# An RWKV and GELU-MLP kernel: the wait between two groups of products on one PSUM tile, through GpSimd instead of a drain

## Chip, core and metric

The kernel runs on one core of a Trainium2 chip. The metric is the device time of one execution in microseconds (us). Before the change its median is 507.57 us over three runs (505.82 to 508.35).

## What is computed

A linear recurrence over 768 time steps for 4 batches and 8 heads of 48 dimensions, and behind it a two-layer MLP with GELU over all 3072 tokens (384 to 2048 to 384). In float32, cut to what matters:

```
for t in range(S):
    kt, vt, rt = k[:, :, t], v[:, :, t], r[:, :, t]
    cur = einsum('bhd,bhe->bhde', u * kt, vt)
    y[:, :, t] = einsum('bhd,bhde->bhe', rt, state + cur)
    state = w * state + einsum('bhd,bhe->bhde', kt, vt)
h = x @ w_in                       # x: y with the heads side by side
out = (0.5 * h * (1 + erf(h / sqrt(2)))) @ w_out
```

## The kernel before

The sequence is cut into 6 chunks of 128 steps, the heads into 4 pairs, so there are 24 groups, a pair in a chunk each. A chunk is halved in time. A group's output is the sum of two kinds of products in PSUM tile Y: those of the old state with r (`old`, line 427) and those of the new keys, that is of the masked scores `Am` with v (`new`, line 437). The scores themselves are products of keys with r (`scores`, line 408, into PSUM tile A); the first eight groups are "direct" and take the step's own key in a second set (`own`, the same line). The products k*v that a state gains over each half go into the upper columns of Y (`gains`, line 419; in the first four groups into another tile). VectorE makes the new state out of the old one and the gains (`state`, line 460), ScalarE and VectorE take the output out of Y as a high and a low part (`keep`, lines 479 and 480).

The MLP runs beside it: per chunk 16 steps, each with 9 big products of 128x512 into tile `Hp` (line 554), GELU on ScalarE (583, 584), a remainder on VectorE (585) and 9 big products into tiles `O` (line 596). Each weight is split into a high part `wh` and a low part `wl` on ScalarE and VectorE (lines 330 to 342), in the first chunk's steps.

After the first four groups, a group's small products come in "visits" between the MLP's big ones (`products`): a visit does `old` and `new` for the group g and `scores` and `gains` for the next group f. A class `Plan` sets the order of all instructions on all engines when the kernel is built, from estimated times and due times; one visit is one entry of it on TensorE, so within a visit the order is as the function `go` writes it. All engines run their queues in that order.

`old` takes its weights from rows that cross over: row half j^h of the array writes into bank h. `new` takes row half h into bank h. So two row halves of the array would write into one bank of Y, and `new` begins with a drain of TensorE (line 433), which waits until all that was issued to TensorE is done. Each `old`, `scores`, `gains` and `new` of a visit is 16 matrix products, 32 records in the trace (8 products for the gains of the last chunk's groups). GpSimd (POOL) multiplies the natural-layout tiles `Nb` of the next group (lines 379, 381, 391), VectorE the transposed ones `Tb` (line 375) and sums rows (line 394); `Nb` and `Tb` have two buffers each and are loaded through SP's queue.

Of the kernel before, what the change touches and what calls it, by code (L numbers as in the profile page):

```python
# [18 lines left out]
B, H, S, D = 4, 8, 768, 48  # L19
# [4 lines left out]
NP = H // 2  # L24
# [3 lines left out]
HALF = 64  # L28
# [17 lines left out]
class Plan:  # L46
# [9 lines left out]
    def add(self, eng, ns, at, fn, r=(), w=()):  # L56
        n = len(self.ops)
        deps = set()
        for x in r:
            deps.add(self.writer.get(x))  # L60
            self.readers.setdefault(x, []).append(n)
        for x in w:
            deps.add(self.writer.get(x))
            deps.update(self.readers.pop(x, ()))
            self.writer[x] = n
        deps -= {None, n}
        self.ops.append((eng, ns, at, fn, deps))
        self.reads.append(set(r))
# [65 lines left out]
def rwkv_gelu_mlp(tc, rkT, rkv, wuT, uN, wmlp, r, k, vT, w, u, out):  # L134
    nc = tc.nc
    with ExitStack() as ctx:
# [11 lines left out]
        AA = psp.tile([128, 2, 512], F32, name="A")  # L148
        YU = psp.tile([128, 2, 512], F32, name="Y")
# [3 lines left out]
        UE = pso.tile([128, 2, 512], F32, name="UE")  # L153
# [194 lines left out]
        U0 = NB * HALF  # L348
        SLOTS = NP + 1
        quarter = lambda x: slice(64 * x, 64 * x + D)  # L350
        heads = lambda x: slice(D * x, D * x + D)
        times = lambda h: slice(64 * h, 64 * h + 64)

        class Group:
            def __init__(g, gi):
                g.gi, g.c, g.p = gi, gi // NP, PAIRS[gi % NP]
                s, i = slot(gi), gi % 2
                g.direct, g.more = gi < DIRECT, g.c < NCH - 1
                g.t, g.T = T[s], f"T{s}"
                g.n = N[s]  # L360
                g.R, g.K, g.V = f"Nr{s}", f"Nk{s}", f"Nv{s}"
                g.kn, g.vn = (g.n[:, 0], g.n[:, 1]) if gi < NP else (g.n[:, 1], g.n[:, 2])
                g.am, g.AM = Am[i], f"Am{i}"
                g.kb, g.KB = KB[i], f"KB{i}"
                g.sums, g.CS = cs[i], f"cs{i}"
                g.x, g.X = (AE, ["O0", "O1"]) if gi < NP and i else (AA, ["A0", "A1"])
                g.y, g.Y = YU, ["Y0", "Y1"]
                g.u, g.U, g.u0 = (UE, ["O2", "H"], i * 256) if gi < NP else (YU, g.Y, U0)
                g.s = [St[0][:, gi % SLOTS], St[1][:, i], St[0][:, (gi + NP) % SLOTS]]
                g.S = [[f"Sa{gi % SLOTS}{x}" for x in range(2)], [f"Sb{i}{x}" for x in range(2)],  # L370
                       [f"Sa{(gi + NP) % SLOTS}{x}" for x in range(2)]]
# [31 lines left out]
        def scores(g, keys=None, col=0):  # L403
            for b in range(NB):
                for h in range(2):
                    for x in range(2):
                        k_ = (g.t[:, 1] if keys is None else keys)[quarter(x), b, times(h)]
                        nc.tensor.matmul(g.x[times(h), x, col + b * HALF:col + (b + 1) * HALF], lhsT=k_,  # L408
                                         rhs=g.t[quarter(x), 0, b, times(h)], start=True, stop=True)

        def own(g):
            scores(g, g.kb, U0)


        def gains(g):
            for b in range(NB):
                for x in range(2):
                    for h in range(2 if g.more else 1):
                        nc.tensor.matmul(g.u[quarter(x), h, g.u0 + b * D:g.u0 + (b + 1) * D], lhsT=g.kn[times(h), b, heads(x)],  # L419
                                         rhs=g.vn[times(h), b, heads(x)], start=True, stop=True)  # L420

        def old(g):
            for b in range(NB):
                for j in range(2):
                    for h in range(1 if g.c == 0 else 0, 2):
                        l = quarter(j ^ h)
                        nc.tensor.matmul(g.y[quarter(j), h, b * HALF:(b + 1) * HALF], lhsT=g.s[h][l, b, :],  # L427
                                         rhs=g.t[l, 0, b, times(h)], start=(b == 0 and not spreads(g)), stop=False,
                                         skip_group_check=True)


        def new(g):
            nc.tensor.drain()
            for b in range(NB):
                for j in range(2):
                    for h in range(2):
                        nc.tensor.matmul(g.y[quarter(j), h, b * HALF:(b + 1) * HALF], lhsT=g.vn[times(h), b, heads(j ^ h)],  # L437
                                         rhs=g.am[times(h), j ^ h, b, :], stop=True, skip_group_check=True,
                                         start=(g.c == 0 and h == 0 and b == 0 and not spreads(g)))


        spreads = lambda g: g.c == 0 and g.p < 3
# [48 lines left out]
        def first_group(gi):  # L491
            g = Group(gi)
            prepare(g)
            add("pe", 600, LATER, lambda: scores(g), r=[g.T], w=g.X)
            add("pe", 600, LATER, lambda: own(g), r=[g.T, f"{g.KB}0", f"{g.KB}1"], w=g.X)
            add("pe", 500, LATER, lambda: (setattr(plan, "hold", True), gains(g)), r=[g.K, g.V], w=g.U)
            state(g, 0, LATER)
            select(g, diag2, "diag", U0)
            select(g, past2, "past", 0)
            if spreads(g):  # L500
                add("pe", 1000, LATER, lambda: gaps(g), r=["spread", "x3h", "x3l"], w=g.Y)
            add("pe", 1000, LATER, lambda: (old(g), new(g)), r=[g.T, g.V, g.AM] + g.S[1], w=g.Y)
            keep(g, LATER)
            state(g, 1, LATER)

        def products(g, f):


            r, w, ns = [], [], 0
            if g:  # L510
                r += [g.T, g.V, g.AM] + g.S[0] + g.S[1]
                w += g.Y
                ns += 1200
            if f:
                r += [f.T, f.K, f.V] + ([f"{f.KB}0", f"{f.KB}1"] if f.direct else [])
                w += f.X + f.U
                ns += 1300 if f.direct else 850

            def go():
                if g:  # L520
                    old(g)
                if f:
                    scores(f)
                    if f.direct:
                        own(f)
                if g:
                    new(g)
                if f:
                    gains(f)

            add("pe", ns, LATER, go, r=r, w=w)
# [175 lines left out]
        for n, x in enumerate(LOADS):  # L707
            at = 10 * n + 1
# [29 lines left out]
        def step_at(m):  # L738
            return FIRST + STEP * min(m, 5 * NJ) + STEP_LAST * max(m - 5 * NJ, 0)

        for G in range(NSTEP + 1):
# [8 lines left out]
            if G % 4 == 0 and G // 4 + NP < NG:  # L750
                gi = G // 4 + NP + 1
                at = step_at(4 * (gi - 1 - NP)) + GROUP_DUE
# [12 lines left out]
        with tc.If(plain[0] < 2 * LP * NP):  # L765
# [5 lines left out]
            g = general.enter_context(tc.tile_pool(name="g", bufs=2))  # L771
# [76 lines left out]
```

## Time and profile before

| | |
|---|---|
| median of 3 runs | 507.57 us (505.82 to 508.35) |
| span of the profiled execution | 507.7 us |
| TensorE products (PE) busy | 486.0 us, 96% |
| TensorE weight loads (PEld) busy | 390.1 us, 77% |
| VectorE (DVE) busy | 243.0 us, 48% |
| ScalarE (ACT) busy | 205.5 us, 40% |
| GpSimd (POOL) busy | 71.6 us, 14% |
| mean granted TensorE clock | 0.971 of full speed |

The span is the time from the first to the last instruction of one profiled execution, on which all rows below rest. Records of products overlap, since they are pipelined and their ends are modelled; distances from start to start are the surer measure. "Idle before" is the time for which an engine had nothing to do, and after the arrow stands what ended it.

### The profile page before, as it was taken

How to read it: one execution, taken by the hardware profiler on the slowest of the kernel's cores; microseconds unless marked ns; L12 is line 12 of the kernel's file. 1: busy time of each engine (PE TensorE's matmuls, PEld its weight loads, DVE VectorE, ACT ScalarE, POOL GpSimd, SP SyncE). 2: the span in 40 equal slices, each digit the busy share in tenths (PEclk: the TensorE clock that was granted, in tenths of full speed). 3: DMA queues.
4: the chain of work that ended last, by engine and by line, in shares of the span. 5: the costliest groups of instructions: out<-in, count | busy, mean ns of one | idle time of the engine just before them, and what ended most of it. 6: DMA issues, size and time to landing. Idle time of an engine off the chain costs nothing.

```text
span 507.7 us, 11458 instructions
## 1 busy us (share of the span) xinstructions
PE 486.0 (96%) x5009; PEld 390.1 (77%) x5009; DVE 243.0 (48%) x366; ACT 205.5 (40%) x435; POOL 71.6 (14%) x80
## 2 busy tenths in 40 slices
PE   7879899999999999999999999999999999999995
PEld 5767677777787787777787787787787787888884
DVE  5869899998345344625254434253433231211111
ACT  3448567755442442442433443433442423322221
POOL 4220101033022022301121120220220200000000
PEclk9568999999999999999999999999999999999999
DMA  7954736622303113403023403033403000100001
GB/s 222 247 196 135 253 118 217 196 87 88 124 24 96 52 43 96 146 1 94 8 88 94 144 3 94 1 94 94 143 5 95 0 13 10 64 1 0 0 1 66
DMA packets 13190, 43.85 MB, mean 86 GB/s; under 512 B 1808, under 2 KB 2192, under 8 KB 13136
## 3 DMA queue, kind: packets, MB, share of 16 engines
q1 hardware_dynamic: 13136, 43.07, 27.3%
q8 instruction: 41, 0.67, 0.6%
q14 instruction: 13, 0.11, 0.1%
HBM read 36.38 MB, written 4.72 MB: 81 GB/s over the span
## 4 chain that ended last, share of the span: by engine, by line
PE 80%; DVE 11%; issue 3%; DMA 3%; ACT 1%; POOL 0%; SPq 0%; DVEq 0%; ACTq 0%; POOLq 0%
PE Hp L554 35%; PE O L596 34%; PE Y L437 3%; PE A L408 3%; PE Y L427 2%; DVE wa L338 2%; DVE wl L342 2%; DVE wa L336 1%; DMA raw<-in_wmlp_dram 1%; PE Y L419 1%; PE Y L596 1%; DVE Am L465 1%; DMA Nb<-in_rkv_dram 1%; DVE gl L585 1%; DVE Tb L375 1%
## 5 line engine op out<-in xcount | busy, mean ns | idle before, releaser
L554 PE MATMUL Hp<-xx,wh 128*128 128x512 f32 x576 | 168.1, 399 | 1.7 <-ACT gf L584 1.0
L585 DVE TENSOR_TENSOR gl<-gf,gh 128x512 fp32r<-128x512 f32 x95 | 71.4, 752 | 193.5 <-ACT gf L584 193.3
L583 ACT ACTIVATE gh<-Hp 128x512 fp32r<-128x512 f32 x95 | 56.9, 599 | 227.7 <-PE Hp L554 227.5
L554 PEld LDWEIGHTS Hp<-xx,wh 128*128 128x128 f32 x576 | 107.0, 189 | 27.9 <-ACT wh L340 1.8
L554 PE MATMUL Hp<-xx,wl 128*128 128x512 f32 x288 | 84.4, 400 | 1.7 <-DVE wl L342 1.7
L596 PE MATMUL O<-gh,wh 128*128 128x512 f32 (+1 forms) x285 | 82.2, 395 | 0.2 <-issue 0.2
L596 PE MATMUL O<-gh,wl 128*128 128x512 f32 (+1 forms) x285 | 80.7, 390 | 0.0
L596 PE MATMUL O<-gl,wh 128*128 128x512 f32 (+1 forms) x285 | 80.7, 390 | 0.0
L554 PEld LDWEIGHTS Hp<-xx,wl 128*128 128x128 f32 x288 | 54.0, 189 | 16.7 <-DVE wl L342 4.1
L596 PEld LDWEIGHTS O<-gh,wh 128*128 128x128 f32 x285 | 52.5, 188 | 13.0 <-issue 0.7
L596 PEld LDWEIGHTS O<-gl,wh 128*128 128x128 f32 x285 | 52.6, 188 | 11.7
L596 PEld LDWEIGHTS O<-gh,wl 128*128 128x128 f32 x285 | 52.5, 188 | 11.6
L584 ACT ACTIVATE gf<-Hp 128x512 f32<-128x512 f32 x96 | 56.9, 593 | 0.0
L379 POOL TENSOR_TENSOR Nb<-Nb 128x384 f32<-128x384 f32 x16 | 18.5, 1159 | 258.1 <-DMA Nb<-in_rkv_dram 215.8
L399 ACT ACTIVATE Am<-diag,cs 128x64 f32<-128x64 f32 x128 | 33.5, 343 | 5.1 <-DVE cs L394 5.0
L381 POOL TENSOR_TENSOR Nb<-Nb,WN 128x384 f32<-128x384 f32 x20 | 27.0, 1349 | 44.2 <-DMA Nb<-in_rkv_dram 42.9
L375 DVE TENSOR_TENSOR Tb<-Tb,E 112x1024 f32<-112x1024 f32 x20 | 25.4, 1269 | 2.0 <-DMA Tb<-in_rkT_dram 1.8
L460 DVE SCALAR_TENSOR_TENSOR Sb<-Sa,E,Y 48x192 f32<-48x192 f32 x40 | 16.5, 413 | 15.4 <-ACT xx L479 9.3
L394 DVE TENSOR_REDUCE cs<-Nb 128x8 f32<-128x384 f32 x16 | 8.8, 552 | 25.5 <-POOL Nb L391 25.5
L479 ACT CAST xx<-Y 112x512 fp32r<-112x512 f32 (+1 forms) x18 | 10.6, 587 | 25.0 <-PE Y L419 17.4
L391 POOL TENSOR_TENSOR Nb<-Nb,u_sb 128x384 f32<-128x384 f32 x16 | 17.7, 1107 | 0.1
L330 ACT ACTIVATE wa<-raw 128x768 f32<-128x768 f32 x16 | 14.6, 912 | 6.5 <-DMA raw<-in_wmlp_dram 4.7
(122 smaller groups left out, 398.8 us busy)
## 6 DMA issues: line engine op xcount, KB each, us to landing
raw<-in_wmlp_dram SPq DMA_DIRECT2D x16, 768.0 KB, 5.0
Nb<-in_rkv_dram SPq DMA_DIRECT2D x16, 576.0 KB, 5.2
Tb<-in_rkT_dram SPq DMA_DIRECT2D x20, 448.0 KB, 3.9
out_dram<-raw SPq DMA_DIRECT2D x5, 768.0 KB, 3.6
xx<-x SPq DMA_DIRECT2D x30, 64.0 KB, 2.7
T<-in_rkT_dram SPq DMA_DIRECT2D x4, 448.0 KB, 5.7
N<-in_rkv_dram SPq DMA_DIRECT2D x4, 384.0 KB, 5.1
Nb<-in_rkv_dram SPq DMA_DIRECT2D x4, 384.0 KB, 6.7
```

Source lines behind the costliest of these rows:

```text
L375: add("dve", sdve(1024), LATER, lambda: nc.vector.tensor_tensor(out=flat, in0=flat, in1=E[:, 0, g.p].rearrange("l h i -> l (h i)").unsquee ...
L379: add("pool", pool(DM), LATER, lambda: nc.gpsimd.tensor_tensor(out=g.n[:, 0], in0=g.n[:, 0], in1=g.n[:, 1], op=ALU.mult), r=[g.K], w=[g.R])
L381: add("pool", pool(DM), LATER, lambda: nc.gpsimd.tensor_tensor(out=g.kn, in0=g.kn, in1=WN[:, g.p].rearrange("s j d -> s (j d)").unsqueeze( ...
L391: add("pool", pool(DM), LATER, lambda: nc.gpsimd.tensor_tensor(out=g.n[:, 0], in0=g.n[:, 0], in1=u_sb[:, g.p, :].unsqueeze(1).to_broadcast ...
L399: add("act", sact(HALF) + 60, LATER, lambda x=x, b=b: nc.scalar.activation(out=g.am[:, x, b, :], in_=diag2, func=AF.Copy, scale=g.sums[:, ...
L408: nc.tensor.matmul(g.x[times(h), x, col + b * HALF:col + (b + 1) * HALF], lhsT=k_, rhs=g.t[quarter(x), 0, b, times(h)], start=True, stop=True)
L460: add("dve", 420, at, lambda l=l, x=x, more=more: nc.vector.scalar_tensor_tensor(out=g.s[h + 1][quarter(1 - x)], in0=g.s[h][l], scalar=E[l ...
L554: nc.tensor.matmul(O[3], lhsT=wt[j][:, 0, k_ * 128:(k_ + 1) * 128], rhs=x[:, a, k_, :], start=start and k_ == ks[0], stop=stop and k_ == k ...
L583: add("act", 600, LATER, lambda: nc.scalar.activation(out=high, in_=O[3], func=AF.Gelu), r=["H"], w=[GH])
L584: add("act", 600, LATER, lambda: nc.scalar.activation(out=gf, in_=O[3], func=AF.Gelu), r=["H"], w=["gf"])
L585: add("dve", sdve(512), LATER, lambda: nc.vector.tensor_tensor(out=low, in0=gf, in1=high.bitcast(F32), op=ALU.subtract), r=["gf", GH], w=[GL])
L596: nc.tensor.matmul(bank(dst)[:, a:b], lhsT=wt[j][:, 1, d * 128:(d + 1) * 128], rhs=gt[:, a:b], start=(j == 0 and n == 0), stop=(j == NJ - ...
```

## The change

In the 19 visits that have a next group, `old` is followed by a no-operation on GpSimd that waits for the last old product (`fence`); the first product of `new` waits for it, and there is no drain. In the 16 of them whose next group isn't direct, `gains` comes before `new`, and it writes into the upper columns of A, not of Y. The four first groups and the last visit keep the drain.

```diff
-                g.u, g.U, g.u0 = (UE, ["O2", "H"], i * 256) if gi < NP else (YU, g.Y, U0)
+                g.u, g.U, g.u0 = (UE, ["O2", "H"], i * 256) if gi < NP else (YU, g.Y, U0) if g.direct else (AA, g.X, U0)
...
         def old(g):
+            i = None
...
-                        nc.tensor.matmul(g.y[quarter(j), h, b * HALF:(b + 1) * HALF], lhsT=g.s[h][l, b, :],
...
+                        i = nc.tensor.matmul(g.y[quarter(j), h, b * HALF:(b + 1) * HALF], lhsT=g.s[h][l, b, :],
...
+            return i
+
+        sync = mybir.DependencyInfo(mybir.DependencyClass.Sync, mybir.DependencyReason.DATA)
+
+        def fence(last):
+
+            at = nc.gpsimd.nop()
+            tc.add_manual_dep(at.ins, last.ins.name, sync, reason="row tiles")
+            return at
+
+        def new(g, passed=None):
+            if passed is None:
+                nc.tensor.drain()
...
+                        if passed is not None:
+                            tc.add_manual_dep(i.ins, passed.ins.name, sync, reason="row tiles")
+                            passed = None
...
             def go():
+                passed = None
                 if g:
-                    old(g)
+                    last = old(g)
+                    passed = fence(last) if f else None
                 if f:
                     scores(f)
                     if f.direct:
                         own(f)
+                    else:
+                        gains(f)
                 if g:
-                    new(g)
-                if f:
+                    new(g, passed)
+                if f and f.direct:
                     gains(f)
```

TensorE's queue in a visit whose next group isn't direct (the end of `old`, then `scores`, `new`, `gains` and the next big products; names in brackets are the semaphores that an instruction waits for). Before:

```order
L427 MATMUL Y<-Tb_106,Sb 48x64
L408 MATMUL A<-Tb_107 64x64 [waits DMAHW1_49]
L408 MATMUL A<-Tb_107 64x64 x15
L437 MATMUL Y<-Am_116,Nb_114 48x64 x16
L419 MATMUL Y<-Nb_115 48x48 [waits DMAHW2_49,Pool_49]
L419 MATMUL Y<-Nb_115 48x48 x15
L596 MATMUL O_563<-gh_124,wh_76 128x512
```

After, at the same place:

```order
L428 MATMUL Y<-Tb_106,Sb 48x64
L408 MATMUL A<-Tb_107 64x64 [waits DMAHW1_49]
L408 MATMUL A<-Tb_107 64x64 x15
L419 MATMUL A<-Nb_115 48x48 [waits DMAHW2_49,Pool_49]
L419 MATMUL A<-Nb_115 48x48 x15
L448 MATMUL Y<-Am_116,Nb_114 48x64 [waits Pool_sequencer_49]
L448 MATMUL Y<-Am_116,Nb_114 48x64 x15
L614 MATMUL O_563<-gh_124,wh_76 128x512
```

The gains moved ahead of `new` and to tile A, and the first product of `new` has a wait for GpSimd's sequencer; neither the drain nor the no-operation is listed.

GpSimd's queue around the same visits (`Nb_114` and `Nb_115` are the two buffers of the natural-layout tile). Before:

```order
L391 TENSOR_TENSOR Nb_114<-Nb_114,u_sb 128x384 [waits DMAHW3_49,DMAHW1_49]
L379 TENSOR_TENSOR Nb_115<-Nb_115 128x384 [waits DMAHW2_49]
L381 TENSOR_TENSOR Nb_115<-Nb_115,WN 128x384 [waits PE_49,Pool_49]
L391 TENSOR_TENSOR Nb_115<-Nb_115,u_sb 128x384
L379 TENSOR_TENSOR Nb_114<-Nb_114 128x384 [waits DMAHW7_49,DVE_49]
```

After:

```order
L391 TENSOR_TENSOR Nb_114<-Nb_114,u_sb 128x384 [waits DMAHW3_49,DMAHW1_49]
L379 TENSOR_TENSOR Nb_115<-Nb_115 128x384 [waits PE_49,DMAHW2_49]
L381 TENSOR_TENSOR Nb_115<-Nb_115,WN 128x384 [waits PE_49,Pool_49]
L391 TENSOR_TENSOR Nb_115<-Nb_115,u_sb 128x384
L379 TENSOR_TENSOR Nb_114<-Nb_114 128x384 [waits PE_49,DMAHW7_49,DVE_49]
```

The order is the same; the no-operation shows as a wait for TensorE that stands between a group's last operation (line 391) and the following group's first (line 379). VectorE's state updates keep their place in its queue and read A in place of Y.

## Rows read from the trace of the kernel before

**Rows 1.** The page: busy times, share of the span, instructions; chain that ended last.

```profile
PE 486.0 (96%) x5009; PEld 390.1 (77%) x5009; DVE 243.0 (48%) x366; ACT 205.5 (40%) x435; POOL 71.6 (14%) x80
...
PE 80%; DVE 11%; issue 3%; DMA 3%; ACT 1%; POOL 0%; SPq 0%; DVEq 0%; ACTq 0%; POOLq 0%
```

**Rows 2.** Stretches: length, busy time of PE, PEld, DVE, ACT, POOL, clock, DMA.

```profile
96.00:126.00 30.00, 28.33 (x236) 21.67 (x236) 28.50 (x39) 17.55 (x34) 8.58 (x6) 1.00 0.41 130
...
215.00:425.00 210.00, 208.81 (x2014) 167.76 (x2012) 77.39 (x117) 75.11 (x183) 31.35 (x28) 1.00 0.20 59
```

**Rows 3.** Timeline (start us, length us, engine, line) of one visit, from its last old product.

```profile
232.74 0.22 PE L427 MATMUL Y<-Tb,Sb 48*48 48x64 f32 x1
232.77 0.65 PE L408 MATMUL A<-Tb 48*64 48x64 f32 x32
233.52 0.52 PEld L437 LDWEIGHTS Y<-Am,Nb 64*48 64x48 f32 x32 [0.24 <-issue]
233.53 0.67 PE L437 MATMUL Y<-Am,Nb 64*48 64x64 f32 x32
234.01 0.54 PE L419 MATMUL Y<-Nb 64*48 64x48 f32 x32
234.48 0.50 PE L596 MATMUL O<-gh,wh 128*128 128x512 f32 x1
```

**Rows 4.** Drain records (ns min/median/max), and loads of `new`, 126 to 425 us.

```profile
L433 PEldq DRAIN  x24: 470/482/1103, 14.4 to 425.4; - x24
...
L437 PEld LDWEIGHTS Y<-Am,Nb 64*48 64x48 f32 x480 | 7.8, 119 | 3.8 <-issue 3.8
```

**Rows 5.** Timeline of a direct visit: scores, own, new.

```profile
93.09 0.65 PE L408 MATMUL A<-Tb 48*64 48x64 f32 x32
...
93.56 0.65 PE L408 MATMUL A<-Tb,KB 48*64 48x64 f32 x32
...
94.31 0.66 PE L437 MATMUL Y<-Am,Nb 64*48 64x64 f32 x32
```

**Rows 6.** Timeline of the first visit, which has no group g: own, gains.

```profile
42.50 0.65 PE L408 MATMUL A<-Tb,KB 48*64 48x64 f32 x32
42.96 0.54 PE L419 MATMUL Y<-Nb 64*48 64x48 f32 x32
```

**Rows 7.** Timeline of the last visit, which has no next group: new, big products.

```profile
426.00 0.67 PE L437 MATMUL Y<-Am,Nb 64*48 64x64 f32 x32
426.59 0.73 PE L596 MATMUL O<-gh,wl 128*128 128x512 f32 x2
```

**Rows 8.** Timeline: GpSimd after a big product; then records of GpSimd's line 215.

```profile
334.40 0.63 PE L554 MATMUL Hp<-xx,wh 128*128 128x512 f32 x2
...
335.14 1.32 POOL L379 TENSOR_TENSOR Nb<-Nb 128x384 f32<-128x384 f32 x1 [15.13 <-PE Hp L554]
...
L215 POOL COPY N<-T x2: 173/174/174, 4.9 to 15.0; 1x1 f32<-1x1 f32 x2
...
L215 POOLq EVENT_SEMAPHORE  x2: 17/17/17, 10.1 to 33.0; - x2
```

**Rows 9.** Timeline from the visit at 192 us to the scores of the next.

```profile
194.51 0.33 SPq L227 DMA_DIRECT2D Nb<-in_rkv_dram  x1
...
202.65 1.01 POOL L381 TENSOR_TENSOR Nb<-Nb,WN 128x384 f32<-128x384 f32 x1
202.72 0.55 DVE L394 TENSOR_REDUCE cs<-Nb 128x8 f32<-128x384 f32 x1 [0.91 <-POOL Nb L391]
203.19 1.55 DVE L375 TENSOR_TENSOR Tb<-Tb,E 112x1024 f32<-112x1024 f32 x1
...
204.80 0.69 PE L408 MATMUL A<-Tb 48*64 48x64 f32 x32 [0.82 <-DVE Tb L375]
```

**Rows 10.** Timeline: the last wait of PE on split weights.

```profile
119.64 0.96 DVE L342 TENSOR_TENSOR wl<-wa,wh 128x768 fp32r<-128x768 f32 x1
...
120.65 0.97 PE L554 MATMUL Hp<-xx,wl 128*128 128x512 f32 x3 [0.75 <-DVE wl L342]
```

More of the change, by code (lines that the diff above doesn't have):

```diff
@@ L426, in old @@
                         l = quarter(j ^ h)
-                        nc.tensor.matmul(g.y[quarter(j), h, b * HALF:(b + 1) * HALF], lhsT=g.s[h][l, b, :],
[L428 to L433, printed above, removed]
+                        i = nc.tensor.matmul(g.y[quarter(j), h, b * HALF:(b + 1) * HALF], lhsT=g.s[h][l, b, :],
+                                             rhs=g.t[l, 0, b, times(h)], start=(b == 0 and not spreads(g)), stop=False,
+                                             skip_group_check=True)
+            return i
[7 more added lines that the diff above has]
+                nc.tensor.drain()
             for b in range(NB):
@@ L436, in new @@
                     for h in range(2):
-                        nc.tensor.matmul(g.y[quarter(j), h, b * HALF:(b + 1) * HALF], lhsT=g.vn[times(h), b, heads(j ^ h)],
-                                         rhs=g.am[times(h), j ^ h, b, :], stop=True, skip_group_check=True,
-                                         start=(g.c == 0 and h == 0 and b == 0 and not spreads(g)))
+                        i = nc.tensor.matmul(g.y[quarter(j), h, b * HALF:(b + 1) * HALF], lhsT=g.vn[times(h), b, heads(j ^ h)],
+                                             rhs=g.am[times(h), j ^ h, b, :], stop=True, skip_group_check=True,
+                                             start=(g.c == 0 and h == 0 and b == 0 and not spreads(g)))
+                        if passed is not None:
+                            tc.add_manual_dep(i.ins, passed.ins.name, sync, reason="row tiles")
+                            passed = None
         spreads = lambda g: g.c == 0 and g.p < 3
```

## Prediction

> **What bounds the kernel now.** I read the page's busy times and chain of waits first [rows 1]: TensorE (PE) is busy 96% of the span, and 80% of the chain that ended last is PE's own. Then the stretches [rows 2]. From 215 to 425 us PE is busy 208.81 of 210.00 us and nothing else is near its limit (VectorE 77.39), so a gap taken out of PE's queue there is taken off the end. From 96 to 126 us it is otherwise: VectorE is busy 28.50 of 30.00 us with splitting weights, and PE stands at 120.65 for `wl` [rows 10]. PE time saved before that wait is mostly given back in it.
>
> Then one visit, row by row [rows 3]. From the start of the score products (232.77) to the first big product (234.48) it takes 1.71 us: scores 0.76, new 0.48, gains 0.47, start to start. The 0.76 holds the drain: `new` starts 0.11 after the scores' last modelled end (233.42). The same scores followed by `own` with no drain take 0.47 [rows 5]. So the drain costs 0.76 - 0.47 = **0.29 us a visit**. Two other views agree in kind: the weight loads of `new` stand idle 3.8 us before 480 loads, 32 a visit, so 15 visits at 0.25 [rows 4]; and the drain's own record of 482 ns [rows 4] lies partly over the scores, so it isn't the price.
>
> **The change part by part.**
> *Drains.* 24 drains are in the trace [rows 4]: 4 first groups, 19 visits with a next group, 1 last visit. The 19 go.
>
> *New order.* In the 16 visits whose next group isn't direct, scores, gains, new, big products follow each other. Scores to gains 0.47 [rows 5]. Gains, when small products follow: the trace doesn't show it. Followed by a big product gains take 0.47 [rows 3]; `new` takes 0.48 before gains but 0.59 before a big product [rows 3, 7], so the step to the big products adds 0.11, and gains cost 0.47 - 0.11 = 0.36. `new` then pays the 0.59. Sum 0.47 + 0.36 + 0.59 = 1.42, against 1.71: **0.29 saved**. If gains kept their 0.47, it would be 0.18; that is the lower bound, and I take 0.29 since it is what the drain alone costs. In the three direct visits the order stays and the gap of 0.28 from `own` to `new` (0.75 start to start against 0.47, [rows 5]) goes.
>
> *The wait through GpSimd.* No such round trip is in the trace; I bound it. The last old product ends at 232.74 + 0.22 = 232.96 [rows 3]; `new` could start by itself at 232.77 + 0.47 + 0.36 = 233.60. So 0.64 us lie over the round trip. Its pieces: PE to GpSimd 0.11 (335.03 to 335.14), a semaphore record on GpSimd's queue 17 ns [rows 8], an engine to PE 0.05 (120.60 to 120.65, [rows 10]). Together 0.18. If the no-op were run by the engine like a one-element copy, 0.17 more [rows 8]: 0.33. Both are hidden; I take 0.18, a cost of nothing, hidden by 32 small products. Upper end: a whole tensor operation of 1.01 [rows 9], 1.17, not hidden. Below nothing it can't go: it only waits.
>
> *GpSimd's queue.* The no-op stands behind the next group's operations, all done before the visit (closest: `L381` ends 203.66 in the visit whose scores start only at 204.80, [rows 9]). Behind it stands the following group's first `Nb` product, which needs a load that starts only after `new`. So nobody new waits.
>
> *The other engines.* Gains now write A: the state update on VectorE waits for them and no longer for ScalarE's cast of Y. That is off PE's path (VectorE is busy 77.39 of 210, [rows 2]), I cost it at nothing. The cast of Y waits for the visit's last section, before and after. The `Nb` load on SP waits for the end of `new`: before 233.53 + 0.67 - 232.77 = 1.43 after the scores' start, after 0.47 + 0.36 + 0.67 = 1.50: 0.07 later. This matters once: after the visit at 192 us the next one comes at 203 us, and PE stands 0.82 for the chain `Nb` load (194.51), GpSimd, reduction, `Tb` (203.19 to 204.74) [rows 9]. There the earlier visit's 0.29 is lost in a longer wait, and 0.07 more.
>
> *Sum.* 15 visits after 126 us [rows 4] x 0.29 = 4.35; less 0.29 and 0.07 for the pair at 192 and 203: 4.0. Of the four visits before (50, 71, 92, 112 us) between 0 and 4 x 0.29 = 1.16 comes through; I take 0.3, near the bottom, because VectorE is busy 28.50 of 30 us before PE's last wait on it. Total **4.3 us**. The profiled execution's span is 507.7, the median of the runs 507.57: they stand 0.1 apart, so I subtract from 507.6: **503.3 us**.
>
> **A rule that speaks against it.** Scores use 48-row weights, gains and new 64-row ones. In the trace `own` (48 rows) goes over to gains (64 rows) with starts 0.46 apart while one section's record lasts 0.65 [rows 6]: PE isn't emptied between them. The Trainium skill, TensorEngine Tiling (Array Packing), Key Properties, says that a change of tiling mode, not merely of tile, drains the TensorE; if 48 to 64 rows were such a change, PE would drain by itself where gains follow scores, and the gain would be about nothing. By that rule the sum would be 0 and the time 507.6; the rows read as one mode throughout, and the trace decides.
>
> **The rivals.**
> 1. *All nineteen pay.* If the early visits' PE time isn't given back (the chain of waits does run through PE in places before 96 us) and the pair at 192 and 203 loses nothing: 19 x 0.29 = 5.5, 502.1. Against it stand [rows 9, 10].
> 2. *Half comes through.* Gains keep 0.47 beside `new`, or PE, held at the wait, loads the first weights of `new` 0.11 late as after a drain [rows 3]: 0.18 a visit, 14 x 0.18 - 0.07 = 2.4, 505.1. For it: no row shows gains before `new`.
> 3. *The wait takes the drain's place.* `new` may start up to 233.89 (234.48 - 0.59) before the visit is as long as now, that is 0.93 after the last old product. A round trip of about 0.9, or a drain that the engine makes by itself as above, gives 507.6: no change. The change could also fail to do what it says; but the order shows the wait for GpSimd's sequencer on the first `new` product of the visits.
> 4. *Slower.* GpSimd's engine takes the no-op in turn like one of its tensor operations: 0.11 + 1.01 + 0.05 = 1.17 after the old products, in each visit. Price 1.17 - 0.93 = 0.24 over now, 15 visits: 3.6, 511.2. It decides from 0.93 on, and passes 0.5% at 0.93 + 2.54 / 15 = 1.10. Against it: the record of 17 ns for a semaphore wait on that queue.
>
> **How the numbers follow.** A measurement of this kernel can tell about 0.5% (2.54 us) from no change: faster is below 505.0, slower above 510.1. Chances: forecast 0.62, rival 1 0.10, rival 2 0.14, rival 3 0.08 (0.03 of it the engine's own drain), rival 4 0.06. The runs of before spread from 505.82 to 508.35, so a median may lie 1 us off. The range 501.5 to 506.5 takes in the forecast, rival 1 and most of rival 2, and leaves out rivals 3 and 4 and some edge: about 0.2. Faster: 0.62 almost whole, 0.10, and under half of 0.14: 0.75. Same: the rest of these and rival 3: 0.18. Slower: 0.07.
>
> **What would show it.** In the profile after: scores to gains 0.47, gains to `new` 0.36, `new` to the big product 0.59, so 1.42 from scores to big product; no idle time of the weight loads before `new` (now 0.24); 5 drain records instead of 24; the waits at 120 us and at 204 us longer by some tenths. Wrong would make it: idle time before `new` that GpSimd ends (rivals 3, 4), gains at 0.47 or more (2), or a gap before gains (the engine's own drain).

## The result and the profile after

| | before | after |
|---|---|---|
| device time, median (lowest to highest) | 507.25 us (505.82 to 508.35) | 502.47 us (498.18 to 503.18) |
| span of the profiled execution | 507.7 us | 500.4 us |
| ratio of the times, 95% interval | | 0.9893 (0.986 to 0.9926) |

The change makes the kernel 1.1% faster, some 5 us; the forecast was 503.3 us. In a second comparison, on another occasion and with more runs (below, the changed kernel again), the ratio was 0.9834 (0.9809 to 0.9859), some 8 us. The two don't agree within their intervals. The experiments show what can move such a comparison, but not which of the two is nearer.

The page of after: busy times, and the chain that ended last. They answer to [rows 1]: PE's share of the chain went from 80% to 83%.

```profile
PE 480.2 (96%) x5009; PEld 386.9 (77%) x5009; DVE 240.8 (48%) x366; ACT 206.6 (41%) x435; POOL 70.8 (14%) x80
...
PE 83%; DVE 9%; DMA 3%; issue 2%; ACT 1%; SPq 0%; POOL 0%; DVEq 0%; ACTq 0%
```

The same stretches as in [rows 2], shifted to the same visits (length, busy PE, weight loads, VectorE, ScalarE, GpSimd, clock, DMA share, GB/s). In the late one PE (TensorE's products) now has no idle time at all: 207.00 of 207.00 us, where before 1.19 of 210 were idle.

```profile
94.00:124.00 30.00, 27.89 (x236) 21.59 (x235) 28.75 (x39) 17.71 (x34) 8.14 (x6) 1.00 0.40 132
210.00:417.00 207.00, 207.00 (x2015) 167.04 (x2013) 75.88 (x117) 75.52 (x183) 30.71 (x29) 1.00 0.20 60
```

One visit of after, as in [rows 3] (start us, length us, engine, line; lines after the changed functions stand 11 to 18 higher in the file than before):

```profile
228.06 0.22 PE L428 MATMUL Y<-Tb,Sb 48*48 48x64 f32 x1
228.10 0.65 PE L408 MATMUL A<-Tb 48*64 48x64 f32 x32
...
228.56 0.54 PE L419 MATMUL A<-Nb 64*48 64x48 f32 x32
...
228.88 0.52 PEld L448 LDWEIGHTS Y<-Am,Nb 64*48 64x48 f32 x32
228.92 0.63 PE L448 MATMUL Y<-Am,Nb 64*48 64x64 f32 x32
...
229.48 0.50 PE L614 MATMUL O<-gh,wh 128*128 128x512 f32 x1
```

Scores to gains 0.46, gains to `new` 0.36, `new` to the big product 0.56 us: 1.38 from scores to big product, where it was 1.71 before. The loads of `new` carry no bracket any more: before, they stood idle for 0.24. From the big product ahead of the visit to the one behind it, start to start, a late visit takes 2.19 us instead of 2.51; the fifteen late visits agree to a hundredth.

The records of the two waits, count and ns (min/median/max), as in [rows 4, 8]: five drains are left (PE's sequencer), and nineteen semaphore waits of 17 ns stand on GpSimd's.

```profile
L444 PEldq DRAIN  x5: 547/1023/1103, 14.7 to 417.4; - x5
...
L438 POOLq EVENT_SEMAPHORE  x19: 17/17/17, 49.8 to 398.3; - x19
```

The two places where the prediction saw gains lost came out differently from each other. First the last wait on `wl` in the timeline of after, which answers to [rows 10] (there 0.75):

```profile
118.58 0.97 PE L572 MATMUL Hp<-xx,wl 128*128 128x512 f32 x3 [1.07 <-DVE wl L342]
```

Then the chain between the pair of visits, which answers to [rows 9]. There PE stood 0.82 us; here the scores carry no bracket. The `Nb` load is issued at 191.48, and GpSimd starts on it 4.07 us later, where it was 5.74 before (194.51 to 200.25).

```profile
191.48 0.33 SPq L227 DMA_DIRECT2D Nb<-in_rkv_dram  x1
195.55 1.02 POOL L379 TENSOR_TENSOR Nb<-Nb 128x384 f32<-128x384 f32 x1 [13.91 <-DMA Nb<-in_rkv_dram]
...
198.60 1.57 DVE L375 TENSOR_TENSOR Tb<-Tb,E 112x1024 f32<-112x1024 f32 x1
...
200.42 0.65 PE L408 MATMUL A<-Tb 48*64 48x64 f32 x32
```

**Where the 7.3 us between the two spans came from.** Four marks cut both traces at the same work: the first visit (41.98 us before, 40.34 after), the first late visit (134.86, 132.79), the last visit (425.22, 417.20) and the end. Ahead of the first visit, after is 1.64 us shorter, though nothing was changed there; PE is busy 31.24 us of it for the same products, where it was 33.03, at a mean granted clock of 0.72 of full speed, where it was 0.67 (the last experiment comes back to this). In the early stage it is 0.43 shorter; in the late stage 5.95, which is 15 x 0.32 = 4.8 and about 1.0 from the vanished wait; behind the last visit after is 0.71 longer, in the last transfers to memory. So the changed visits explain 5 of the 7.3; the rest is differences between two executions or the wait on a load, and the experiments ask which.

### The profile page after: what moved, and what is told of

Read it like the earlier page. It is cut to its first block, busy times and chain, and to the rows that moved or that the text cites. A ratio compares the mean times of both kernels' runs of the same rounds, so it can differ in the third digit from the quotient of the medians.

```text
span 500.4 us, 11449 instructions
## 1 busy us (share of the span) xinstructions
PE 480.2 (96%) x5009; PEld 386.9 (77%) x5009; DVE 240.8 (48%) x366; ACT 206.6 (41%) x435; POOL 70.8 (14%) x80
## 4 chain that ended last, share of the span: by engine, by line
PE 83%; DVE 9%; DMA 3%; issue 2%; ACT 1%; SPq 0%; POOL 0%; DVEq 0%; ACTq 0%
PE Hp L572 37%; PE O L614 35%; PE Y L428 3%; PE A L408 2%; PE Y L448 2%; DVE wa L338 2%; DVE wl L342 2%; DMA T<-in_rkT_dram 1%; DVE wa L336 1%; DMA raw<-in_wmlp_dram 1%; PE Y L614 1%; DVE Am L479 1%; PE A L419 1%; DVE gl L603 1%; DVE T L375 1%
## 5 line engine op out<-in xcount | busy, mean ns | idle before, releaser
L603 DVE TENSOR_TENSOR gl<-gf,gh 128x512 fp32r<-128x512 f32 x95 | 69.3, 729 | 192.7 <-ACT gf L602 192.5
L379 POOL TENSOR_TENSOR Nb<-Nb 128x384 f32<-128x384 f32 x16 | 19.7, 1230 | 254.9 <-DMA Nb<-in_rkv_dram 244.5
L381 POOL TENSOR_TENSOR Nb<-Nb,WN 128x384 f32<-128x384 f32 x20 | 25.1, 1256 | 41.2 <-DMA Nb<-in_rkv_dram 40.0
L342 DVE TENSOR_TENSOR wl<-wa,wh 128x768 fp32r<-128x768 f32 x16 | 16.6, 1037 | 1.3 <-ACT wh L340 1.2
L479 DVE COPY_PREDICATED Am<-past,A 128x512 f32<-128x512 uint32 x22 | 16.2, 736 | 1.7 <-PE A L419 1.4
```

The lines of the kernel that those rows point to most:

```text
L342: add("dve", sdve(n), LATER, lambda: nc.vector.tensor_tensor(out=both(wl), in0=af, in1=both(wh).bitcast(F32), op=ALU.subtract), r=[A_, f"w ...
L379: add("pool", pool(DM), LATER, lambda: nc.gpsimd.tensor_tensor(out=g.n[:, 0], in0=g.n[:, 0], in1=g.n[:, 1], op=ALU.mult), r=[g.K], w=[g.R])
L381: add("pool", pool(DM), LATER, lambda: nc.gpsimd.tensor_tensor(out=g.kn, in0=g.kn, in1=WN[:, g.p].rearrange("s j d -> s (j d)").unsqueeze( ...
L479: add("dve", 722, LATER, lambda: nc.vector.copy_predicated(out=g.am, mask=mask.bitcast(U32).unsqueeze(1).unsqueeze(1).to_broadcast([C, 2, ...
L603: add("dve", sdve(512), LATER, lambda: nc.vector.tensor_tensor(out=low, in0=gf, in1=high.bitcast(F32), op=ALU.subtract), r=["gf", GH], w=[GL])
```

## The experiments

All ratios are against the kernel before, run beside the experiment on the same chip: the first four experiments on one occasion, the next four on another, the last alone.

**The changed kernel again**, nothing edited.

> The changed kernel once more, for a second trace. In its first trace PE did not wait at all in the visit at 200 us, where the kernel before waited 0.82 us for the chain Nb load, GpSimd, reduction, Tb; the Nb load of that chain took 3.94 us instead of 5.61. Theory A: the length of that one load decides, and it changes from run to run: here the wait is max(0, load - 4.2 us), so anything from 0 to 1.5 us. Theory B: the change itself shortened the chain: the wait is 0 again and the load again near 4 us. Time by both 501.5 to 503.5.

Measured: 500.57 us, a little under the 501.5 to 503.5 expected, ratio 0.9834 (0.9809 to 0.9859). The late visits are the same to a hundredth, but for the one at 200 us. The `Nb` load took 4.37 us from issue to landing, and from the old products to the scores it is 0.69 us instead of 0.48: 0.21 lost. That fits theory A (4.37 less 4.2), but alone it doesn't exclude B; the table further down does.

**Drain kept, gains moved.** Order and bank as in the change, the drain as before.

```diff
-                    passed = fence(last) if f else None
+                    passed = None
```

> The order and the bank of the change (k*v products ahead of the new keys' products, into A), but every visit keeps its drain, now between gains and new. Theory: the drain is the whole price; it costs about 0.28 us of idle PE wherever it stands, so a visit is 2.47 to 2.51 us as before and the time is 506.5 to 507.5. Rival: the new order itself carries the gain (fewer sections in which the state and the cast wait for each other): visits of 2.2 to 2.3 us or a gap that the gains hide, 502 to 504.

Measured: 508.03 us, ratio 0.9998 (0.9973 to 1.0023): no gain at all (the kernel before took 508.74 beside it). Its visit, timeline:

```profile
228.95 0.65 PE L408 MATMUL A<-Tb 48*64 48x64 f32 x32
...
229.41 0.54 PE L419 MATMUL A<-Nb 64*48 64x48 f32 x32
...
230.08 0.52 PEld L448 LDWEIGHTS Y<-Am,Nb 64*48 64x48 f32 x32 [0.26 <-issue]
230.09 0.66 PE L448 MATMUL Y<-Am,Nb 64*48 64x64 f32 x32
...
230.68 0.73 PE L614 MATMUL O<-gh,wh 128*128 128x512 f32 x2
```

The idle time of the loads, 0.24 in [rows 3], is 0.26 here, only behind the gains instead of behind the scores. Gains to `new` is 0.68 where the changed kernel has 0.36, and `new` to the big product 0.59 instead of 0.56. So the drain costs 0.32 ahead of `new` here, behind the gains, where it cost 0.29 behind the scores, and 0.03 inside `new` at either place: it waits for whatever was issued last.

**Wait through GpSimd, gains left in place.** The other half of the change: gains behind `new` and in Y, as before.

```diff
-                g.u, g.U, g.u0 = ... else (YU, g.Y, U0) if g.direct else (AA, g.X, U0)
+                g.u, g.U, g.u0 = ... else (YU, g.Y, U0)
...
                     if f.direct:
                         own(f)
-                    else:
-                        gains(f)
                 if g:
                     new(g, passed)
-                if f and f.direct:
+                if f:
                     gains(f)
```

> The wait through GpSimd in place of the drain, but the k*v products stay behind the new keys' products and in Y, so only the scores lie between. Cover: new could start 0.95 us after the visit's start, the last old product ends 0.67 after it: 0.28. Theory: the round trip is 0.18 to 0.28, hidden even so; scores to new 0.47, new 0.48, gains 0.47, a visit of 2.2 us and 502 to 503 us. Rival: the round trip is longer than 0.28, say 0.4: 0.12 us of idle time ahead of new in 16 visits, released by GpSimd, 504.3 us; at 0.56 all of the gain is gone, 507.

Measured: 499.9 us, under the 502 to 503 expected as the changed kernel is under its own range; ratio 0.9832 (0.9807 to 0.9858), the same as the changed kernel beside it (0.9834). Timeline:

```profile
224.94 0.65 PE L408 MATMUL A<-Tb 48*64 48x64 f32 x32
...
225.35 0.53 PEld L448 LDWEIGHTS Y<-Am,Nb 64*48 64x48 f32 x32
225.41 0.63 PE L448 MATMUL Y<-Am,Nb 64*48 64x64 f32 x32
...
225.86 0.54 PE L419 MATMUL Y<-Nb 64*48 64x48 f32 x32
```

`new` follows the scores after 0.47 and has no idle time: a cover of 0.28 us is enough, so the round trip isn't longer than that. The time is all in the wait; that k*v products come between bought nothing that can be measured.

**Only the late visits changed.** The three direct visits (49, 70, 91 us) keep the drain.

```diff
-                    passed = fence(last) if f else None
+                    passed = fence(last) if f and not f.direct else None
```

> The change only in the visits whose next group is not direct; the three direct visits (49, 70 and 91 us) keep the drain. Theory: what these three save (0.33 us each, 1.0 in all) is mostly given back at PE's waits for wl at 98 and 119 us: 0.0 to 0.4 us over the changed kernel, 502.3 to 502.9, and the wait at 119 us is shorter by the rest than its 1.07. Rival: nothing is given back: 1.0 over, 503.4.

Measured: 501.64 us, ratio 0.9876 (0.9838 to 0.9913), 1.1 over the changed kernel beside it, with intervals that overlap. By size this is the rival's 1.0. But its trace doesn't tell the two apart, since it lost time in two waits, one on `wl` and one on `Tb`:

```profile
115.05 0.99 POOL L379 TENSOR_TENSOR Nb<-Nb 128x384 f32<-128x384 f32 x1 [11.81 <-DMA Nb<-in_rkv_dram]
115.17 1.69 DVE L342 TENSOR_TENSOR wl<-wa,wh 128x768 fp32r<-128x768 f32 x1
...
116.92 0.95 PE L572 MATMUL Hp<-xx,wl 128*128 128x512 f32 x3 [1.80 <-DVE wl L342]
...
189.80 0.33 SPq L227 DMA_DIRECT2D Nb<-in_rkv_dram  x1
...
200.27 0.69 PE L408 MATMUL A<-Tb 48*64 48x64 f32 x32 [1.09 <-DVE Tb L375]
```

I expected the wait on `wl` to be shorter than 1.07; it is 1.80. The 0.73 more is VectorE's operation that makes `wl`: it takes 1.69 us here, where it takes 0.96 in the trace of after. GpSimd's operation on `Nb` began 0.12 us ahead of it here, and 0.35 behind it there (117.92 and 117.57). In all eleven traces this operation of VectorE takes 0.93 to 0.96 us in the 149 cases in which no tensor operation of GpSimd runs at its start. In 23 of the 27 cases in which one does, it takes 1.35 to 1.74; in the other four GpSimd's takes 2.7 to 4.8 instead of 1.0. So here, too, it is the time at which an `Nb` load lands that counts, and the experiment is inconclusive for the early visits. The second wait says something: here the visits on both sides are those of the changed kernel, and the wait is back, after an `Nb` load of 6.15 us.

**All drains replaced.** The last five too, where nothing lies between old and `new`: the bare price of the wait.

```diff
-                    passed = fence(last) if f else None
+                    passed = fence(last)
...
-            add("pe", 1000, LATER, lambda: (old(g), new(g)), r=[g.T, g.V, g.AM] + g.S[1], w=g.Y)
+            add("pe", 1000, LATER, lambda: new(g, fence(old(g))), r=[g.T, g.V, g.AM] + g.S[1], w=g.Y)
```

> The changed kernel with the last five drains (four first groups, last visit) replaced by the same GpSimd no-operation, where nothing lies between the old products and the new ones: the uncovered price of the wait. With the drain new starts 0.78 us after old in the last visit, 0.11 after the last modelled end. Theory: a round trip of 0.18 us: new starts 0.80 to 0.87 after old, a few hundredths worse than the drain; in the first groups the same, unless the no-operation stands behind GpSimd's work for a later group, up to 1 us. Time within 0.5 us of the changed kernel, 500 to 502.5. Rival: a round trip of 0.5 us, which 32 small products would hide as well: new 1.15 after old, 2 us in all.

Measured: 499.8 us, ratio 0.9869 (0.9843 to 0.9896). The end of old and the start of `new` in its last visit, and the records of the wait:

```profile
414.33 0.22 PE L428 MATMUL Y<-Tb,Sb 48*48 48x64 f32 x1
...
414.68 0.52 PEld L448 LDWEIGHTS Y<-Am,Nb 64*48 64x48 f32 x32 [0.28 <-POOLq L438]
414.68 0.66 PE L448 MATMUL Y<-Am,Nb 64*48 64x64 f32 x32
```

```profile
L438 POOLq EVENT_SEMAPHORE  x24: 17/17/17, 14.6 to 414.6; - x24
```

`new` starts 0.80 after old's start, 0.13 after the last modelled end (414.55 to 414.68); with the drain 0.78 and 0.11. In the four first groups the gap is 0.12 to 0.21 us with the wait and 0.08 to 0.09 with the drain. So uncovered, the wait through GpSimd is slightly the worse of the two. Its whole use is that other products may run meanwhile.

**A longer wait, still covered.** The no-operation replaced by a fill of 128x384.

```diff
-            at = nc.gpsimd.nop()
+            at = nc.gpsimd.memset(slack, 0.0)
```

> The no-operation replaced by a real GpSimd instruction, a fill of 128x384 in a scratch tile, estimated at 0.42 us from the fills of 128x512 (530 ns) and 128x128 (205 ns) in the trace. Round trip 0.11 + 0.42 + 0.05 = 0.58 us, under the cover of 0.64. Theory: no idle time ahead of new, visits of 2.19 us, 500 to 502.5 as the changed kernel. Rival: the cover is smaller than worked out or a GpSimd instruction costs more than its record: an idle time of 0.1 to 0.3 us ahead of new in 16 visits, 502 to 506.

Measured: 499.76 us, ratio 0.988 (0.9848 to 0.9912), visits of 2.19. Timeline, with the fill on GpSimd:

```profile
225.74 0.42 POOL L439 MEMSET slack<- 128x384 f32 x1 [17.15 <-PE Y L429]
...
225.94 0.54 PE L420 MATMUL A<-Nb 64*48 64x48 f32 x32
...
226.25 0.52 PEld L449 LDWEIGHTS Y<-Am,Nb 64*48 64x48 f32 x32
226.30 0.63 PE L449 MATMUL Y<-Am,Nb 64*48 64x64 f32 x32
```

The fill ends at 226.16 and `new` starts by itself at 226.30, without idle time. A wait of 0.56 us (0.09 and 0.05 for the two hops, by the next experiment, and the fill's 0.42) is hidden here. With the gains left in place only 0.28 is covered, so by this sum it would show there; that was not run.

**A longer wait than the cover.** Two fills of 128x512.

```diff
-            at = nc.gpsimd.nop()
-            tc.add_manual_dep(at.ins, last.ins.name, sync, reason="row tiles")
+            at = None
+            for _ in range(2):
+                at = nc.gpsimd.memset(slack, 0.0)
+                tc.add_manual_dep(at.ins, last.ins.name, sync, reason="row tiles")
```

> The no-operation replaced by two fills of 128x512 in turn, 2 x 0.53 us. Round trip 0.11 + 1.06 + 0.05 = 1.22 us, 0.58 over the cover of 0.64 and 0.29 over the break-even of 0.93 after the last old product. Theory: gains to new 0.94 instead of 0.36, idle time that GpSimd ends, a visit of 2.75 to 2.8 us against 2.51 before; 15 late visits x 0.58 = 8.7 us over the changed kernel, 3.6 to 4.4 over the kernel before: 509 to 513. Rival: PE's queue hides more of it (weights loaded ahead), or the early stage takes more of it away: under 507.

Measured: 512.48 us, ratio 1.0122 (1.0088 to 1.0155): slower than before. Timeline:

```profile
231.10 0.65 PE L409 MATMUL A<-Tb 48*64 48x64 f32 x32
231.37 1.11 POOL L441 MEMSET slack<- 128x512 f32 x2 [17.16 <-PE Y L429]
...
231.56 0.54 PE L420 MATMUL A<-Nb 64*48 64x48 f32 x32
...
232.53 0.52 PEld L451 LDWEIGHTS Y<-Am,Nb 64*48 64x48 f32 x32 [0.55 <-POOL slack L441]
232.53 0.66 PE L451 MATMUL Y<-Am,Nb 64*48 64x64 f32 x32 [0.43 <-POOL slack L441]
```

Gains to `new` 0.97 (0.94 expected), a visit of 2.84 (2.75 to 2.8 expected). The fills start 0.09 after the last old product's end (231.28) and `new` starts 0.05 after theirs (232.48): the two hops of the prediction, 0.11 and 0.05, measured. The whole wait is 0.09 + 1.11 + 0.05 = 1.25, and it makes `new` 0.61 later than in the changed kernel, so 0.64 of it is covered, as worked out. This is rival 4 made real, and dearer than it was priced: 0.33 a visit over the kernel before, and 6.2 us in all, where a wait of 1.17 was priced at 0.24 and 3.6. Had GpSimd's engine taken the no-operation in turn, at the length of a tensor operation, the change would have been slower.

**The wait on ScalarE.** The same no-operation on the engine that has the gelus.

```diff
-            at = nc.gpsimd.nop()
+            at = nc.scalar.nop()
```

> The no-operation on ScalarE instead of GpSimd. There it stands ahead of the two gelus of the big products just before the visit, which start 0.1 us into the visit now (227.72 in a visit that starts at 227.61) and would start only after the last old product, some 0.6 us later; the second gelu then ends at about 229.43, and the first big product after the visit, which writes the bank that it reads, starts at 229.48. Theory: the gelus move by 0.6 us and that just fits, 0 to 0.1 us of waiting a visit: 500 to 503. Rival: a no-operation that costs what stands behind it: PE waits for Hp by 0.1 to 0.3 us in 19 visits, 502.5 to 506.

Measured: 501.24 us, ratio 0.989 (0.9864 to 0.9916), visits of 2.19 to 2.20. ScalarE's timeline in the visit that starts at 227.34:

```profile
228.15 0.60 ACT L601 ACTIVATE gh<-Hp 128x512 fp32r<-128x512 f32 x1 [3.83 <-PE Y L428]
228.65 0.59 ACT L602 ACTIVATE gf<-Hp 128x512 f32<-128x512 f32 x1
```

The gelu now waits for the old products and starts 0.81 after the visit's start, where it was 0.11 (227.72 in after): 0.70 us later for what stands behind the waiting instruction. PE doesn't notice, and more easily than I had worked out: the first big products after the visit write O [the visit of after, above], not the bank that the gelu reads.

**The kernel before again**, nothing edited.

> The kernel before once more, for a second trace of two things that its first trace showed once: the first visit started at 41.98 us (in the nine traces of its relatives since, 37.98 to 40.34), and PE waited 0.82 us at 204 us after an Nb load of 5.61 us. Theory: both belong to the execution and not to the kernel: the first visit starts anywhere from 38 to 42 us, and the wait follows the load, about load minus 4.5 to 4.8 us and not under 0 (the visit before it is 0.32 us longer than in the changed kernel, which gives the load that much more time). From the first visit to the end 465 to 466 us, less what the wait is shorter than 0.82. Rival: the kernel before always starts late and always waits 0.8 us: 41 to 42.5 us and 0.7 to 0.9.

Measured: 505.67 us, one run, span 504.0. Its first visit starts at 37.24 us, not at 41.98: 4.7 us between two executions of one kernel, ahead of anything that the change touches, and as much as the change brings. It lies outside the 38 to 42 expected; that range was too narrow already, since the 37.98 to 40.34 behind it leave out the 35.57 us of the kernel with all drains replaced. The stretch up to the first visit, before and before again (columns as in [rows 2]):

```profile
0.00:41.98 41.98, 33.03 (x616) 26.95 (x616) 29.32 (x51) 19.04 (x38) 11.00 (x30) 0.67 0.71 211
0.00:37.24 37.24, 28.36 (x617) 22.88 (x617) 29.01 (x51) 19.25 (x38) 15.74 (x30) 0.82 0.79 246
```

PE is idle for the same time in both, 8.95 and 8.88 us. The difference is in its busy time, 4.67 us longer for the same products, at a granted clock of 0.67 against 0.82, which is a mean over its two levels (1.2 and 2.4 GHz). In the first 10 us, with PE busy 7.38 and 6.96 of them, both have the upper level; behind them it is at the lower one for part of the time in both. From 45 to 480 us all eleven traces have the upper level. What made it differ was not tried.

From the first visit to the end it takes 466.7 us, against 465.7: as much more as the chain of [rows 9] loses more (1.99 and 1.01, below). Its wait is longer, not shorter:

```profile
189.85 0.33 SPq L227 DMA_DIRECT2D Nb<-in_rkv_dram  x1
...
196.93 1.01 POOL L379 TENSOR_TENSOR Nb<-Nb 128x384 f32<-128x384 f32 x1 [17.73 <-DMA Nb<-in_rkv_dram]
...
198.26 0.47 PE L554 MATMUL Hp<-xx,wh 128*128 128x512 f32 x1 [0.46 <-DMA xx<-x]
...
199.52 1.54 DVE L375 TENSOR_TENSOR Tb<-Tb,E 112x1024 f32<-112x1024 f32 x1
...
201.12 0.69 PE L408 MATMUL A<-Tb 48*64 48x64 f32 x32 [1.09 <-DVE Tb L375]
```

The `Nb` load, issued at 189.85, took 6.95 us to land; the transfers behind it were late too, and PE stood for `xx<-x` as well. The loss is 1.99 us in all, where load minus 4.5 to 4.8 gives 2.15 to 2.45. All eleven traces of this chain, by the length of that one load; "left" is the time from its landing to the start of the next visit, less what PE lost between them; "lost" is how much longer than 0.48 it is from the start of the old products to that of the scores, and what PE lost ahead of them:

| kernel | `Nb` load, us | left, us | lost, us |
|---|---|---|---|
| after | 3.94 | 4.51 | 0 |
| fill of 128x384 | 4.02 | 4.44 | 0 |
| wait on ScalarE | 4.14 | 4.31 | 0.01 |
| all drains replaced | 4.15 | 4.30 | 0.01 |
| after, again | 4.37 | 4.09 | 0.21 |
| wait alone, gains in place | 4.52 | 4.27 | 0.04 |
| drain kept, gains moved | 4.79 | 3.67 | 0.55 |
| two fills | 4.87 | 3.56 | 0.64 |
| before | 5.61 | 3.19 | 1.01 |
| late visits only | 6.15 | 2.30 | 1.28, and 0.26 ahead |
| before, again | 6.95 | 1.85 | 1.28, and 0.71 ahead (0.46 of it idle for `xx<-x`) |

The loss follows the load and not the kernel: nothing up to 4.2 us, then some tenths, over 1 us from 5.6 on. That is theory A. By the time that is left the order has no exception: where the wait stands alone, `new` ends earlier, and the load is issued 0.35 us sooner in the visit, so 4.52 costs less there than 4.37 elsewhere. Whether the loads are longer by chance alone in the kernels with a drain (4.79, 5.61 and 6.95, against 3.94 to 6.15 in the eight others) can't be told from three traces; this stays open.

## Why the prediction was right, and where it wasn't

**The price of the drain** was read rightly. 0.29 us a visit was forecast as the difference of two rows [rows 3, 5]; 0.32 came. Scores to gains (0.46 or 0.47) and gains to `new` 0.36 came out as worked out; the missing 0.03 is `new` itself, which passes on to the big product after 0.56, where I carried 0.59 over from a visit with a drain [rows 7]. After a drain the section is 0.03 longer (0.48 against 0.45 in the direct visits too). 15 x 0.03 = 0.45 us mis-sized.

**The wait through GpSimd** costs nothing, as forecast. The two fills measure its hops (0.09 and 0.05), the uncovered case its sum: 0.12 to 0.21 us after the last modelled end, 0.18 forecast. The longer waits bear out the cover of 0.64: a fill of 0.42 is hidden, and of the two fills' wait 0.64 is.

**The engine's own drain by a change of tiling mode** (rival 3) didn't come. From scores, with 48-row weights, to gains, with 64, the starts lie 0.46 apart, and no bracket stands there [the visit of after]. The Trainium skill, TensorEngine Tiling (Array Packing), Key Properties, says that a change of tiling mode drains the TensorE. No drain shows at this pair of shapes. Either the two count as one mode or the rule doesn't hold for them; no run here tells which, and the trace decides.

**The early visits** were forecast to keep 0.3 us of 1.16. From the first visit to the first late one the three traces with a drain everywhere (before, before again, drain kept) take 92.88, 92.94 and 92.71 us, and five with the wait in all visits 92.45, 91.97, 91.53, 92.18 and 92.30: means 92.84 and 92.09. The sixth, with all drains replaced, takes 93.80; PE stands 1.12 us for a gelu in its first visit, which starts earliest of all. So some 0.75 of 1.3 came through (0.47 with the sixth), where the five alone lie up to 0.9 apart: the size is rough. The mechanism is there, since the last wait on `wl` grew by the whole gain of the visit ahead of it (0.70 to 0.75 with the drain, 1.07 in all six traces with an unlengthened or hidden wait in every visit), but not all of what the other early visits save is given back. I took a busy share over 30 us for a statement about all four visits.

**The pair of visits at 192 and 203 us** is the step that failed. I took 0.36 off for a wait that would grow, and in the trace of after it was gone, a gain of 1.0 instead. The reasoning that a shorter visit leaves the load less time holds: from the issue of the load to the next visit it is 8.80 us before (194.51 to 203.31) and 8.45 after (191.48 to 199.93), 0.35 less. But the length of the wait was read from one execution, as if it belonged to the kernel. It belongs to a transfer that took 3.94 to 6.95 us in eleven traces.

**The sum.** By rows of all traces: 15 x 0.32 = 4.8 in the late visits and some 0.75 in the early ones, 5.6 us, plus whatever the load does to the pair. The forecast of 4.3 was some 1.3 too small, on the side that its range allowed for. The measured 5 and 8 us lie on both sides of this, so it is in part luck that the first comparison came out only 0.8 us from the forecast. The late stage by itself is steadier: from the first late visit to the last, the three traces with a drain take 290.21 to 291.33 us, and the six with a hidden wait in every visit 284.41 to 284.83. The start is one place that can move a comparison: the same kernel reached its first visit 4.7 us apart in two executions, with a granted clock of 0.67 and 0.82 up to it. But that this made the comparisons differ is not shown. The median of the kernel before was 507.25, 508.74 and 506.25 us in the three timed comparisons.

**A better version?** The wait alone (0.9832), all drains replaced (0.9869), and the fill (0.988) lie between the two measurements of the changed kernel (0.9834 and 0.9893) or at their edge. None can be told from it. Of the change itself, the wait is what counts; the moved gains only add cover, 0.64 us instead of 0.28.

## What to carry to other kernels

A drain waits for everything that was issued, also for products that nobody has to wait for; a wait through another engine's queue names the last product that matters, and lets the rest run. It is not cheaper by itself (0.13 against 0.11 us after the last product here), so it pays only with independent work to put over it. It also holds up what stands behind it on the queue that it uses: 0.70 us for the gelu on ScalarE, which did no harm here; on a queue whose next instruction is due it would cost, though no run shows that.

Price such a step by the difference of two neighbouring sections in one trace, which held to 0.03 us; but don't put a wait for a transfer into the sum from one execution: look at it in several, or give it both signs.

## What the runs showed that I had not expected

- The section behind a drain is 0.03 us longer than without it, beside the 0.29 ahead of it (`new` to the big product 0.59 and 0.56).
- A real GpSimd instruction works as a fence at its own length plus 0.09 us before it and 0.05 behind; the bare semaphore wait stands there with a record of 17 ns.
- The same 576 KB load, at the same place of the program, took 3.94 to 6.95 us in eleven traces, and the first visit started between 35.6 and 42.0 us, with a mean granted clock of 0.67 to 0.87 up to it. Why they differ was not tried.
- VectorE's operation for `wl` took 0.93 to 0.96 us, and 1.35 to 1.74 where a tensor operation of GpSimd had begun before it; this alone made a wait of PE 0.73 longer in one trace.
